# A fused attention and MLP kernel on one core: another recorded order of all instructions, from other planning constants

## The chip, the cores and the metric

One Trainium2 chip, one of its cores. The metric is device microseconds of one execution; the kernel before was executed three times (707.9, 707.91 and 710.89 us, median 707.91). The profile is of one more execution of 703.5 us, whose span from the first to the last instruction is 701.8 us.

## The reference, cut to what matters

Two stages in float32. A recurrence over 768 tokens for 4 x 8 heads of dimension 40:

```python
for t in range(S):
    y[:, :, t] = einsum('bhd,bhde->bhe', r_t, state)
    Sa = einsum('bhde,bhe->bhd', state, a_t)
    state = state * w_t[:, :, None, :] - einsum('bhd,bhe->bhde', Sa, b_t) + einsum('bhd,bhe->bhde', v_t, k_t)
```

and on its output, as 3072 tokens of 320 numbers, a bilinear MLP: `((x @ w1) * (x @ w2)) @ w3 @ w_out`, with `w1`, `w2` of 320 x 1024, `w3` of 1024 x 1024 and `w_out` of 1024 x 320. The weights come as float64.

## The kernel before, in words

The 768 tokens are cut into 12 chunks of 64 (numbered 0 to 11), and the 32 heads into two groups of 16. A chunk goes through these steps, each a function:

- `load` brings the decays and keys (tile `fm`, four buffers: two chunks) and `a` (tile `lh`). `scale` forms running products of the decays (a scan, L441), their inverses, and multiplies them into `lh` (L453) and into `fm` (L465).
- `causal` makes the products of all pairs of tokens (L490) and masks them with GpSimd selects (L508). `solve` inverts a triangular system on VectorE: pairs of a product (L548) and a reduction (L552), some 19 us in a row for a chunk. `join` puts the inverse together with two TensorE steps, L623 and L630; between them ScalarE copies the first result (`JP`).
- `pairs` (L667, and GpSimd selects L677) and `tokens` (L694) prepare the other operands.
- `rec` carries the state over a chunk, for each group: TensorE L718 and L725, then L733, four VectorE products L738, TensorE L745, VectorE L771 (state) and L790 (output), TensorE L778 (the state turned round for the next chunk).
- `gather` moves the output into the layout of the MLP by twelve DMAs, and `mlp` runs 24 TensorE units for a chunk: 16 of 8 matmuls (L842) and 8 of 6 (L868), each near 1 us. VectorE splits the input (`xs`, L828) and multiplies (L856); the low part `gl` (L859) is made on VectorE or GpSimd.

Before any `mlp` all weights have to be converted: 31 `convert` calls on VectorE (L333, L337, L341 each), `split` into high and low parts (L382, L394, on GpSimd), and `product`, which folds `w3` and `w_out` into one matrix on TensorE (L404). The first `mlp` reads the key `W12`, which is written when all of `w1` and `w2` are split.

The order of the work is not that of the code. Every step is recorded by `op(engine, cost, due, fn, r, w, two=...)`: the planned cost, a due time, what it reads and writes. `Order.place` then places all operations by a list schedule: on each engine the operation that could start first by the plan, among equals the one due first; on TensorE, among those within `sl` of the first, the one with the smallest due time, less `kp` when it needs no change of the array's mode. `two=True` marks operations of VectorE and GpSimd that the plan lets run only one at a time. The recorded closures are then called in the placed order, and each engine works through its own list in that order. The due times come from the numbers `T0`, `T` and `P`; `ON` says chunk by chunk whether L453 (`lh`), L465 (`xs`) and L859 (`gl`) run on GpSimd (`p`) or on VectorE (`d`). A cost in the plan is no wait on the chip: it only sets the order.

## Time and profile before

| | |
|---|---|
| median of 3 executions | 707.91 us |
| profiled execution | 703.5 us, span 701.8 us |
| TensorE busy | 588.2 us (84%) |
| VectorE busy | 562.1 us (80%) |
| ScalarE busy | 427.6 us (61%) |
| GpSimd busy | 199.5 us (28%) |
| mean granted TensorE clock | 0.952 |

TensorE is busy for a small part of the first 80 us, while VectorE is nearly full from 20 us on; from about 200 us on both are nearly full, and in the last 70 us only TensorE is. A busy share over the whole span therefore says little; the kernel has to be read stage by stage.

### The profile page before, as it was taken

To read this page: it belongs to the slowest core of one execution; us is meant where nothing else is said; L and a number is where in the kernel's file an instruction comes from. 1 tells how busy PE (TensorE), PEld (TensorE's weight loads), DVE (VectorE), ACT (ScalarE), POOL (GpSimd) and SP (SyncE) were. 2 spreads that over 40 slices of the span, in tenths; PEclk is the share of its full clock that TensorE was granted. 3 is DMA by queue.
4 is the path that set the end of the run, shared out by engine and by line. 5 is a ranking of instruction groups with operands and counts; after the bars stand their busy time and mean duration, and the time that the engine had idled before them with its cause. 6 is when DMAs were issued, how large, how long until landed. Compare 5 with 4: busy or idle time off the path is not lost.

```text
span 701.8 us, 22309 instructions
## 1 busy us (share of the span) xinstructions
PE 588.2 (84%) x9458; PEld 522.5 (74%) x9458; DVE 562.1 (80%) x989; ACT 427.6 (61%) x927; POOL 199.5 (28%) x186
## 2 busy tenths in 40 slices
PE   1331597475899799998999899999899999999996
PEld 1321475244798698897988889889888999899996
DVE  7899899989899888979979879699697797963321
ACT  2781575648567386693694765856848569464231
POOL 4370214204240010330221632426427143200200
PEclk9999998785899899998999999999999899999999
DMA  7940575152331321413314313233133250210011
GB/s 177 227 125 23 183 193 149 60 161 79 75 71 43 80 69 53 104 44 90 85 40 104 71 48 84 69 99 88 34 95 71 50 127 22 64 32 22 21 24 23
DMA packets 61090, 57.56 MB, mean 82 GB/s; under 512 B 29560, under 2 KB 52600, under 8 KB 60984
## 3 DMA queue, kind: packets, MB, share of 16 engines
q1 hardware_dynamic: 60984, 56.07, 31.4%
q8 instruction: 76, 1.25, 0.8%
q14 instruction: 30, 0.25, 0.1%
HBM read 47.40 MB, written 3.93 MB: 73 GB/s over the span
## 4 chain that ended last, share of the span: by engine, by line
DVE 47%; PE 29%; DMA 10%; ACT 6%; issue 6%; SPq 1%; POOL 1%; DVEq 0%; ACTq 0%; POOLq 0%
PE bank L842 12%; DVE tmp L548 8%; DMA fm<-in_fmx_dram 8%; DVE xu L738 6%; PE bank L868 5%; DVE mf L337 3%; DVE fm L441 3%; DVE ab L552 3%; DVE DG L552 2%; ACT JP L212 2%; DVE ab L522 2%; DVE Tp L552 2%; PE bank L745 2%; ACT TT L212 2%; PE bank L725 2%
## 5 line engine op out<-in xcount | busy, mean ns | idle before, releaser
L842 PE MATMUL bank<-xs,W 128*128 128x256 f32 x1536 | 207.4, 289 | 0.9 <-ACT TT L212 0.7
L842 PEld LDWEIGHTS bank<-xs,W 128*128 128x128 f32 x1536 | 189.4, 191 | 8.3 <-issue 1.8
L677 POOL TENSOR_SCALAR_AFFINE_SELECT xu<-xu 64x512 f32<-64x512 f32 x48 | 33.9, 707 | 176.5 <-ACT xu L212 168.9
L212 ACT ACTIVATE xu<-bank 64x256 f32<-64x256 f32 (+2 forms) x184 | 70.8, 436 | 11.2 <-PE bank L667 5.0
L856 DVE TENSOR_TENSOR ga<-bank,ga 128x512 f32<-128x512 f32 x48 | 32.9, 687 | 54.3 <-PE bank L842 39.6
L212 ACT ACTIVATE JP<-bank 32x512 f32<-32x512 f32 x120 | 60.4, 503 | 11.4 <-PE bank L490 7.0
L508 POOL TENSOR_SCALAR_AFFINE_SELECT lh<-lh 64x512 f32<-64x512 f32 x48 | 35.7, 744 | 108.8 <-ACT lh L212 105.9
L868 PE MATMUL bank<-W3h,gh 128*128 128x320 f32 x192 | 62.7, 327 | 0.0
L745 PE MATMUL bank<-xu,bk 128*40 128x104 f32 (+1 forms) x768 | 51.8, 271 | 12.3 <-DVE xu L738 11.7
L404 PE MATMUL bank<-wof,w3f 128*128 128x320 f32 x128 | 45.0, 508 | 18.8 <-DVE w3f L341 18.8
L738 DVE TENSOR_TENSOR xu<-bank,mask_h 64x416 f32<-64x416 f32 x96 | 56.2, 585 | 4.4 <-PE bank L733 2.1
L868 PE MATMUL bank<-W3l,gh 128*128 128x320 f32 x192 | 59.6, 310 | 0.0
L868 PE MATMUL bank<-W3h,gl 128*128 128x320 f32 x192 | 59.3, 309 | 0.0
L453 POOL TENSOR_TENSOR lh<-lh,fm 104x1024 f32<-104x1024 f32 x20 | 43.9, 2194 | 46.3 <-DVE fm L441 39.1
L745 PEld LDWEIGHTS bank<-xu,bk 128*40 128x40 f32 (+1 forms) x768 | 39.8, 125 | 22.8 <-DVE xu L738 19.3
L725 PE MATMUL bank<-xu,lh 104*64 104x104 f32 (+2 forms) x768 | 44.1, 267 | 11.8 <-POOL xu L677 7.2
L490 PE MATMUL bank<-lh,fm 40*64 40x64 f32 x1536 | 33.1, 244 | 22.7 <-DVE fm L465 14.5
L404 PEld LDWEIGHTS bank<-wof,w3f 128*128 128x128 f32 x128 | 27.7, 225 | 32.8 <-DVE w3f L341 15.2
L725 PEld LDWEIGHTS bank<-xu,lh 104*64 104x64 f32 (+2 forms) x768 | 38.0, 144 | 17.0 <-POOL xu L677 7.8
L490 PEld LDWEIGHTS bank<-lh,fm 40*64 40x64 f32 x1536 | 29.7, 157 | 27.3 <-issue 22.5
L859 POOL TENSOR_TENSOR gl<-ga,gh 128x512 fp32r<-128x512 f32 x24 | 32.6, 1360 | 60.8 <-ACT gh L212 60.8
L212 ACT ACTIVATE SB<-bank 40x320 f32<-40x320 f32 x44 | 18.9, 429 | 50.8 <-PE bank L778 50.3
(99 smaller groups left out, 1223.6 us busy)
## 6 DMA issues: line engine op xcount, KB each, us to landing
fm<-in_fmx_dram SPq DMA_DIRECT2D x24, 627.2 KB
raw<-in_w3t_dram SPq DMA_DIRECT2D x16, 512.0 KB
rv<-in_rv_dram SPq DMA_DIRECT2D x48, 160.0 KB
raw<-in_w_dram SPq DMA_DIRECT2D x8, 512.0 KB
lh<-in_fma_dram SPq DMA_DIRECT2D x48, 80.0 KB
xu<-in_vt_dram SPq DMA_DIRECT2D x48, 80.0 KB
out_dram<-o SPq DMA_DIRECT2D x48, 80.0 KB
xr<-y SPq DMA_DIRECT2D x72, 40.0 KB
```

Source lines behind the costliest of these rows:

```text
L212: act.activation(out_, in_, AF.Copy, scale=scale)
L404: pe.matmul(out=pt.t[:, 0:DM], lhsT=w[:, j], rhs=wof[:, j], start=(j == 0), stop=(j == NJ - 1))
L453: e.tensor_tensor(out=lh.t[0:104], in0=lh.t[0:104], in1=gam(c, g)[:, :, 0:C].unsqueeze(1).to_broadcast(full), op=ALU.mult)
L490: pe.matmul(out=bank(ab)[64 * x:64 * x + 64, p], lhsT=X[r, p, x], rhs=lh.t[r, ab, p], start=True, stop=True)
L508: pool.affine_select(out=lh.t[q, ab], in_=lh.t[q, ab], pattern=[[0, NP], [1, C]], compare_op=ALU.is_gt, fill=0.0, base=0, channel_multipli ...
L548: dve.tensor_tensor(out=scratch(*shape), in0=x().to_broadcast([128, *shape]), in1=y().to_broadcast([128, *shape]), op=ALU.mult)
L552: dve.tensor_reduce(out=out_(), in_=scratch(*shape), axis=mybir.AxisListType.X, op=ALU.add)
L725: pe.matmul(out=view(hp[h])[64 * ab:64 * ab + 64, u], lhsT=lh.t[k, ab, HP * h + u], rhs=xu.t[k, ab, HP * h + u], start=True, stop=True)
L738: dve.tensor_tensor(out=xu.t[64 * ab:64 * ab + 64, ab, k:NP:2], in0=view(us[ab])[r], in1=mask_h[r].unsqueeze(1).to_broadcast([64, HP, N]), ...
L745: pe.matmul(out=q(r, p), lhsT=bk.t[:, p, r], rhs=xu.t[:, ab, p], start=(c == 0), stop=True, skip_group_check=True)
L842: pe.matmul(out=pt.t[:, TOK * x:TOK * x + TOK], lhsT=WT[k][:, cs], rhs=xs.t[:, z], start=(n == 0), stop=(n == 7))
L868: pe.matmul(out=pt.t[:, 0:DM], lhsT=l.t[:, j, ts], rhs=W3[r][:, j], start=(j == 0 and n == 0), stop=(j == NJ - 1 and n == 2))
```

## The change

Only numbers and marks that the plan reads; no operation is added or removed. The due times and the choice of engine:

```diff
-T0, T = 44.72, 43.86
-P = dict(w0=17.72, ws=3.55, ld=127.38, sc=59.49, ca=49.87, so=11.77, sp=31.26, jo=5.02, pa=19.94, tk=0.13, rg=7.05,
-         ga=24.69, ml=80.68, kp=7.95, mt=26.56, mg=18.0, sl=0.28, kw=0.05)
+T0, T = 51.29, 43.14
+P = dict(w0=24.52, ws=3.55, ld=120.72, sc=65.76, ca=50.03, so=18.07, sp=32.97, jo=0, pa=14.07, tk=0, rg=6.24,
+         ga=21.36, ml=83.8, kp=5.81, mt=26.61, mg=18.52, sl=0.56, kw=2.39)
 
-ON = dict(ws="p", lh="pppddppppppp", xs="dpppdpdpdppd", gl="ddddpppppdpd")
+ON = dict(ws="p", lh="pdpddppdpppp", xs="dpppdpdpdddp", gl="pdpdppppdpdp")
```

Planned costs of some twenty operations move by a few per cent, the product of the first seven `solve` pairs gets a factor, and the two GpSimd selects lose their mark:

```diff
-            op("pool", 0.83, due + 6, f3, w=[(lh, ab)], two=True)
+            op("pool", 0.67, due + 6, f3, w=[(lh, ab)])
...
-            steps.append((0.16 + n / 960, f1, False))
+            steps.append((0.15 + slow * n / 960, f1, False))
...
-                 lambda s=s: A8(s).unsqueeze(2), (4, n, n))
+                 lambda s=s: A8(s).unsqueeze(2), (4, n, n), 1.75)
...
-            op("pool", 0.85, due + 2, lambda q=q, ab=ab: pool.affine_select(
+            op("pool", 0.67, due + 2, lambda q=q, ab=ab: pool.affine_select(
...
-                fill=0.0, base=0, channel_multiplier=-1), w=[(xu, "g", ab)], two=True)
+                fill=0.0, base=0, channel_multiplier=-1), w=[(xu, "g", ab)])
```

Counted over the 12 chunks, `ON` moves the `lh` products from 20 on GpSimd and 4 on VectorE to 16 and 8, the `xs` products from 14 and 10 to 12 and 12, and the `gl` subtractions from 24 and 24 to 32 and 16.

What that does to the order, at three places. First VectorE around the last weight conversion (the last L341). Before, that conversion stands ahead of all VectorE work of chunk 1's recurrence (L738, L771, L790):

```order
L333 TENSOR_SCALAR mf_145<-raw_141 128x512
L337 SCALAR_TENSOR_TENSOR mf_145<-raw_141,mf_145 128x512
L341 SCALAR_TENSOR_TENSOR mf_145<-raw_141,mf_145 128x512
L738 TENSOR_TENSOR xu_105<-bank_134,mask_h 64x4x104
L738 TENSOR_TENSOR xu_105<-bank_131,mask_h 64x4x104
```

Now the first group's share of that recurrence stands ahead of the last two conversions (the last one begins in the last row here):

```order
L738 TENSOR_TENSOR xu_105<-bank_131,mask_h 64x4x104
L738 TENSOR_TENSOR xu_105<-bank_130,mask_h 64x4x104
L738 TENSOR_TENSOR xu_105<-bank_131,mask_h 64x4x104
L738 TENSOR_TENSOR xu_105<-bank_130,mask_h 64x4x104
L564 TENSOR_TENSOR tmp<-DG 128x128
L333 TENSOR_SCALAR mf_146<-raw_140 128x512
...
L771 TENSOR_TENSOR st_110<-bank_132,fm_94 104x160
L790 TENSOR_TENSOR y_111<-bank_132,fm_94 104x4x64
...
L333 TENSOR_SCALAR mf_145<-raw_141 128x512
```

Counted over the whole list up to the last L341, nothing moved behind it, and two L453 (chunk 1's), four L738, two L771, two L790 and nine steps of chunk 2's `solve` moved ahead of it. Up to the first L828, the `xs` split that the first MLP needs, again nothing moved behind, and what moved ahead is two L453, four L738, two L771, two L790, five L548 and five L552 of `solve`, and one L436, one L441 and one L453 of chunk 3. On TensorE all of chunk 1's recurrence and the preparation of chunk 2 (L667, L694) now stand ahead of the first L842.

Second, TensorE in the recurrence of chunk 2, first group. Before, L745 follows L733 at once, though the four VectorE products L738 stand between them:

```order
L725 MATMUL bank5_135<-xu0_105,lh0_96 64x104 x8
L733 MATMUL bank2_132<-hs0_109,TT0_115 64x104
...
L733 MATMUL bank4_134<-hs0_109,TT0_115 64x104
L745 MATMUL bank0_130<-xu0_105,bk0_107 40x104 x8
L745 MATMUL bank1_131<-xu0_105,bk0_107 40x104 x8
L778 MATMUL bank3_133<-ident_64,st0_110 40x104 x4
```

Now three MLP units (18 L868) stand between them:

```order
L725 MATMUL bank5_135<-xu0_105,lh0_96 64x104 x8
L842 MATMUL bank2_132<-xs0_1519,W12_0_89 128x256 x2
...
L733 MATMUL bank4_134<-hs0_109,TT0_115 64x104
L868 MATMUL bank5_135<-W3h_87,gh0_1517 128x320
...
L868 MATMUL bank5_135<-W3h_87,gl0_1518 128x320
L745 MATMUL bank0_130<-xu0_105,bk0_107 40x104 x8
L745 MATMUL bank3_133<-xu0_105,bk0_107 40x104 x8
```

From chunk 2 on every group of every chunk has at least three other pieces there now; before, the first groups of chunks 2 and 4 had none.

Third, TensorE in `join` of chunk 6. Before, L630 follows L623 at once (in chunks 8 and 9 too):

```order
L842 MATMUL bank4_134<-xs0_1403,W12_4_1153 128x256 x2
L623 MATMUL bank0_130<-TDX0_102,JP0_113 32x32 x32
L630 MATMUL bank0_130<-TDX0_102,JP0_113 32x32 x32
L842 MATMUL bank5_135<-xs0_1403,W12_0_89 128x256 x2
L842 MATMUL bank5_135<-xs0_1403,W12_2_90 128x256
```

Now three MLP units stand between the two steps:

```order
L623 MATMUL bank2_132<-TDX0_102,JP0_113 32x32 x32
L842 MATMUL bank5_135<-xs0_1519,W12_0_89 128x256 x2
...
L842 MATMUL bank5_135<-xs0_1519,W12_4_1229 128x256 x2
L868 MATMUL bank0_130<-W3h_87,gh0_1517 128x320
...
L868 MATMUL bank0_130<-W3h_87,gl0_1518 128x320
L630 MATMUL bank2_132<-TDX0_102,JP0_113 32x32 x32
```

No chunk from 2 on has the two steps side by side any more. At the end of the list TensorE runs 48 MLP units behind the last L745 now, 41 before.

## Rows read from the trace of the kernel before

**Rows 1.** The page of the profile: the span, and two engines' busy tenths in 40 equal slices.
```profile
span 701.8 us, 22309 instructions
...
PE   1331597475899799998999899999899999999996
...
DVE  7899899989899888979979879699697797963321
```

**Rows 2.** The table of stretches: length, then busy us (instructions) of PE, PEld, DVE, ACT and POOL, the granted clock, the DMA share and GB/s.
```profile
160.00:180.00 20.00, 13.45 (x193) 10.65 (x194) 18.06 (x37) 14.74 (x30) 8.87 (x7) 0.50 0.17 52
300.00:350.00 50.00, 47.60 (x799) 43.06 (x798) 42.60 (x80) 31.85 (x68) 12.47 (x11) 0.93 0.29 67
```

**Rows 3.** VectorE in order of time, 182 to 197 us: start, length, then the instruction, and in brackets the idle time before it. The first row is the first MLP's `xs`, the others are steps of `solve`.
```profile
181.97 0.96 DVE L828 TENSOR_TENSOR xs<-xr,xs 128x768 fp32r<-128x768 f32 x1 [0.26 <-ACT xs L825]
182.84 0.41 DVE L548 TENSOR_TENSOR tmp<-Tp,ab 128x256 f32<-128x256 f32 x1
183.29 0.43 DVE L552 TENSOR_REDUCE ab<-tmp 128x32 f32<-128x256 f32 x1
186.50 0.69 DVE L548 TENSOR_TENSOR tmp<-Tp,ab 128x512 f32<-128x512 f32 x1
```

**Rows 4.** TensorE in order of time from the first MLP unit on. Of the eight rows up to 207 us that belong to chunk 1's recurrence and chunk 2's preparation (L733, L745, L778, L667, L694) the first and the last are shown.
```profile
186.11 1.21 PE L842 MATMUL bank<-xs,W 128*128 128x256 f32 x8
187.25 0.94 PE L733 MATMUL bank<-hs,TT 64*64 64x104 f32 x32
...
206.04 0.57 PE L694 MATMUL bank<-ident,fm 104*128 104x104 f32 x4
```

**Rows 5.** Groups of instructions by line: busy us and mean ns of one, then the idle time before them.
```profile
L453 POOL TENSOR_TENSOR lh<-lh,fm 104x1024 f32<-104x1024 f32 x20 | 43.9, 2194 | 46.3 <-DVE fm L441 39.1 <-issue 3.6 <-DMA xr<-y 3.3
L859 POOL TENSOR_TENSOR gl<-ga,gh 128x512 fp32r<-128x512 f32 x24 | 32.6, 1360 | 60.8 <-ACT gh L212 60.8
L465 DVE TENSOR_TENSOR fm<-fm,gi 104x1024 f32<-104x1024 f32 x10 | 12.2, 1223 | 0.3
L859 DVE TENSOR_TENSOR gl<-ga,gh 128x512 fp32r<-128x512 f32 x24 | 16.8, 700 | 11.5 <-ACT gh L212 11.5
L738 DVE TENSOR_TENSOR xu<-bank,mask_h 64x416 f32<-64x416 f32 x96 | 56.2, 585 | 4.4 <-PE bank L733 2.1
L790 DVE TENSOR_TENSOR y<-bank,fm 104x256 f32<-104x256 f32 x48 | 19.1, 416 | 3.2 <-PE bank L745 3.2
L771 DVE TENSOR_TENSOR st<-bank,fm 104x160 f32<-104x160 f32 x44 | 13.5, 318 | 3.0 <-PE bank L745 2.9
L436 DVE TENSOR_SCALAR_CACHE_REDUCE fm<-fm 104x520 f32<-104x520 f32 x24 | 16.6, 691 | 12.6 <-DMA fm<-in_fmx_dram 12.5
L337 DVE SCALAR_TENSOR_TENSOR mf<-raw,mf 128x512 uint32<-128x512 uint32 x31 | 29.9, 964 | 1.0
L571 DVE TENSOR_TENSOR Tp<-tmp,DG 128x128 f32<-128x128 f32 x12 | 9.3, 779 | 0.4
L441 DVE TENSOR_TENSOR_SCAN fm<-fm,first 104x520 f32<-104x520 f32 x24 | 36.1, 1505 | 0.6
```

**Rows 6.** VectorE in order of time, 39 to 52 us, and two later rows of lines met there.
```profile
39.56 1.02 DVE L461 SCALAR_TENSOR_TENSOR gi<-gt,gi 104x512 f32<-104x512 f32 x1
40.50 7.36 DVE L441 TENSOR_TENSOR_SCAN fm<-fm,first 104x520 f32<-104x520 f32 x1
48.79 2.98 DVE L571 TENSOR_TENSOR Tp<-tmp,DG 128x128 f32<-128x128 f32 x1
...
75.76 0.69 DVE L337 SCALAR_TENSOR_TENSOR mf<-raw,mf 128x512 uint32<-128x512 uint32 x1
...
181.31 0.40 DVE L571 TENSOR_TENSOR Tp<-tmp,DG 128x128 f32<-128x128 f32 x1
188.65 1.24 DVE L441 TENSOR_TENSOR_SCAN fm<-fm,first 104x520 f32<-104x520 f32 x1
```

**Rows 7.** GpSimd in order of time, 39 to 52 us.
```profile
39.05 2.04 POOL L677 TENSOR_SCALAR_AFFINE_SELECT xu<-xu 64x512 f32<-64x512 f32 x2
...
42.29 2.16 POOL L453 TENSOR_TENSOR lh<-lh,fm 104x1024 f32<-104x1024 f32 x1
...
49.37 2.15 POOL L453 TENSOR_TENSOR lh<-lh,fm 104x1024 f32<-104x1024 f32 x1
```

**Rows 8.** TensorE in order of time: the rows behind 210 us with an idle time of over a microsecond before them.
```profile
232.29 4.51 PE L745 MATMUL bank<-xu,bk 128*40 128x104 f32 x32 [4.26 <-DVE xu L738]
323.77 4.51 PE L745 MATMUL bank<-xu,bk 128*40 128x104 f32 x32 [2.08 <-DVE xu L738]
402.93 1.20 PE L630 MATMUL bank<-TDX,JP 32*32 32x32 f32 x64 [1.96 <-ACT JP L212]
448.49 1.20 PE L630 MATMUL bank<-TDX,JP 32*32 32x32 f32 x64 [1.48 <-ACT JP L212]
495.16 1.20 PE L630 MATMUL bank<-TDX,JP 32*32 32x32 f32 x64 [1.74 <-ACT JP L212]
539.82 1.20 PE L630 MATMUL bank<-TDX,JP 32*32 32x32 f32 x64 [1.54 <-ACT JP L212]
```

**Rows 9.** The table of stretches again (columns as in rows 2), for the four stretches behind 200 us with a granted clock of 0.50.
```profile
231.30:238.10 6.80, 5.65 (x50) 3.92 (x54) 5.90 (x12) 0.43 (x1) 0.00 (x0) 0.50 0.03 5
...
323.50:330.30 6.80, 6.37 (x42) 4.94 (x43) 6.03 (x16) 0.00 (x0) 0.00 (x0) 0.50 0.10 15
...
449.80:453.20 3.40, 3.40 (x72) 3.17 (x75) 1.45 (x2) 2.23 (x5) 1.06 (x1) 0.50 0.00 0
...
541.90:548.70 6.80, 6.80 (x113) 6.32 (x111) 1.03 (x2) 5.96 (x13) 1.30 (x2) 0.50 0.11 33
```

**Rows 10.** The chain that ended last, its end: start, length, piece.
```profile
657.84 8.68 PE bank L842 x72
666.52 7.05 PE bank L868 x48
673.56 15.24 PE bank L842 x128
688.81 7.06 PE bank L868 x48
```

More of the change, by code (lines that the diff above doesn't have):

```diff
@@ L342, in f6 @@
                                      op0=ALU.logical_shift_right, op1=ALU.bitwise_or)
-        op("sp", 0.4, due - 8, f1, w=[raw], dma=2.0)
-        op("act", 0.72, due, f2, r=[raw], w=[sq])
-        op("act", 0.72, due, f3, w=[sq])
-        op("dve", 0.52, due, f4, r=[raw], w=[mf], two=True)
-        op("dve", 0.72, due, f5, r=[raw], w=[mf], two=True)
-        op("dve", 0.74, due, f6, r=[raw, "conv"], w=[mf] if dst is None else [mf, *w], two=True)
+        op("sp", 0.35, due - 8, f1, w=[raw], dma=2.5)
+        op("act", 0.8, due, f2, r=[raw], w=[sq])
+        op("act", 0.76, due, f3, w=[sq])
+        op("dve", 0.42, due, f4, r=[raw], w=[mf], two=True)
+        op("dve", 0.7, due, f5, r=[raw], w=[mf], two=True)
+        op("dve", 0.7, due, f6, r=[raw, "conv"], w=[mf] if dst is None else [mf, *w], two=True)
         return mf
@@ L384, in split @@
             op("act", 0.65, due, lambda: copy(WT[k][:, cs], mf.t.bitcast(F32)), r=[mf, *over], w=[("W", k, f)])
-            both(ON["ws"], 1.35, 0.62, due, f2, r=[mf, *over], w=[("W", k, f)])
+            both(ON["ws"], 1.28, 0.69, due, f2, r=[mf, *over], w=[("W", k, f)])
             return due
@@ L393, in split @@
                    r=[mf, *over], w=[key])
-            both(ON["ws"], 1.35, 0.62, due, lambda e, q=q, dst=dst: e.tensor_tensor(
+            both(ON["ws"], 1.28, 0.69, due, lambda e, q=q, dst=dst: e.tensor_tensor(
                 out=WT[4][64:128, dst], in0=mf.t[q].bitcast(F32), in1=WT[4][q, dst], op=ALU.subtract), r=[mf, *over], w=[key])
@@ L408, in product @@
         op("act", 0.45, due, lambda: copy(W3[0][:, ib], pt.t[:, 0:DM]), r=[pt], w=[("W3", ib)])
-        op("dve", 0.43, due, lambda: dve.tensor_tensor(out=W3[1][:, ib], in0=pt.t[:, 0:DM], in1=W3[0][:, ib],
+        op("dve", 0.48, due, lambda: dve.tensor_tensor(out=W3[1][:, ib], in0=pt.t[:, 0:DM], in1=W3[0][:, ib],
                                                      op=ALU.subtract), r=[pt], w=[("W3", ib)])
@@ L423, in load @@
         fm, lh = fm_[c, g], lh_[c, g] = slot("fm"), slot("lh")
-        op("sp", 0.4, due, lambda: sp.dma_start(out=fm.t, in_=fmx[c, g]), w=[(fm, "g"), (fm, "x")], dma=2.5)
+        op("sp", 0.4, due, lambda: sp.dma_start(out=fm.t, in_=fmx[c, g]), w=[(fm, "g"), (fm, "x")], dma=3.0)
         for ab in range(2):
@@ L468, in scale @@
         op("dve", 0.7, due, f1, w=[G])
-        op("dve", 1.26, due, f2, w=[G], two=True)
+        op("dve", 1.24, due, f2, w=[G], two=True)
         op("act", 0.63, due + 1, f3, r=[G], w=[gi])
-        op("act", 0.71, due + 1, f4, w=[gi])
-        both(ON["lh"][c], 2.35, 1.16, due + 1, f5, r=[G], w=[(lh, 0), (lh, 1)])
+        op("act", 0.76, due + 1, f4, w=[gi])
+        both(ON["lh"][c], 2.2, 1.22, due + 1, f5, r=[G], w=[(lh, 0), (lh, 1)])
         op("dve", 0.71, due + 2, f6, r=[G, gi], w=[gt], two=True)
         op("dve", 0.73, due + 2, f7, r=[gt], w=[gi], two=True)
-        both(ON["xs"][c], 2.6, 1.16, due + 3, f8, r=[gi], w=[(fm, "x")])
+        both(ON["xs"][c], 2.38, 1.22, due + 3, f8, r=[gi], w=[(fm, "x")])
     def causal(c, g, due):
@@ L541, in scratch, with dots @@
             return tmp[:, 0:n].rearrange(f"p ({' '.join(names)}) -> p {' '.join(names)}", **dict(zip(names, shape)))
-        def dots(out_, x, y, shape):
+        def dots(out_, x, y, shape, slow=1.0):
             n = shape[0] * shape[1] * shape[2]
@@ L830, in mlp @@
         parts = [(xr, i) for i in range(12)] if first else []
-        op("act", 0.9, due - 3, f1, r=[*parts, "W12"], w=[(xs, "h")])
+        op("act", 0.98, due - 3, f1, r=[*parts, "W12"], w=[(xs, "h")])
         op("dve", 0.98, due - 2, f2, r=[(xs, "h"), *parts], w=[(xs, "l")], two=True)
@@ L855, in mlp @@
                 else:
-                    op("dve", 0.65, t, lambda a=a, pt=pt: dve.tensor_tensor(out=a.t, in0=wide(pt), in1=a.t, op=ALU.mult),
+                    op("dve", 0.69, t, lambda a=a, pt=pt: dve.tensor_tensor(out=a.t, in0=wide(pt), in1=a.t, op=ALU.mult),
                        r=[pt], w=[a])
             op("act", 0.64, t, lambda a=a, j=j: copy(gh.t[:, j:j + 2], a.t), r=[a], w=[(gh, j)])
-            both(ON["gl"][c % NCH], 1.35, 0.62, t + 1, lambda e, a=a, j=j: e.tensor_tensor(
+            both(ON["gl"][c % NCH], 1.3, 0.69, t + 1, lambda e, a=a, j=j: e.tensor_tensor(
                 out=gl.t[:, j:j + 2], in0=a.t, in1=gh.t[:, j:j + 2], op=ALU.subtract), r=[a, (gh, j)], w=[(gl, j)], of=op)
```

2 lines of the change are left out of this document (1 added, 1 removed).

## The prediction, made before the changed kernel ran

> **What bounds the kernel now.** The page comes first, its row of slices above all [rows 1]. In the first fifth VectorE is nearly full and TensorE mostly idle: the weights are being converted, and no MLP can start. From about 200 us on both are nearly full: 47.60 us of 50 on TensorE and 42.60 on VectorE between 300 and 350 us [rows 2]. In the last five slices only TensorE works. So the span is the time at which the first MLP unit starts (186.11 us [rows 4]), plus the TensorE work left by then, plus what TensorE loses after it, plus 6 us behind its last matmul. The chain of waits shows that the last MLPs run without a gap: 8.68 + 7.05 + 15.24 + 7.06 = 38.0 us up to 695.9 us [rows 10].
>
> What TensorE loses after the start is read from two views. In order of time, six rows have over a microsecond of idle before them: two before L745, which waits for the four L738 on VectorE, and four before L630, which waits for ScalarE's copy of L623's result: 4.26 + 2.08 + 1.96 + 1.48 + 1.74 + 1.54 = 13.1 us [rows 8]. The table of stretches shows the granted clock at 0.50, the lower of its two levels (1.2 of 2.4 GHz), four times, twice beginning in such a gap and twice some 2 us behind one [rows 8, 9]: 5.65 + 6.37 + 3.40 + 6.80 = 22.2 us of work that would take half of that, so 11.1 us lost. Together 24.2 us that hang on six gaps.
>
> **The change, part by part.** The work is the same; I go by which work stands ahead of which.
>
> *VectorE ahead of the first MLP.* What moved ahead of L828 is costed by kind. Two L453 of chunk 1 and one of chunk 3 at 1.22 us make 3.7 (the time is that of L465 on VectorE, also 104x1024, 1223 ns [rows 5]); four L738 at 0.585, two L771 at 0.318 and two L790 at 0.416 make 3.8 [rows 5]; one L436 0.69 [rows 5], one L441 1.24 [rows 6]; four `solve` pairs at 0.41 + 0.43 and one pair at about 0.69 + 0.69 make 4.7 [rows 3]. The sum is 14.1 us. Before, L828 starts at 181.97 [rows 3], on a VectorE that is busy 18.06 of 20 us just then [rows 2], so nothing hides this: L828 moves to 196.1, ends at 197.1, and since all TensorE work that stood behind the first unit now stands ahead of it, the first L842 comes at once: 197.1 instead of 186.1, **+11.0**.
>
> *TensorE ahead of the first MLP.* Chunk 1's recurrence and chunk 2's preparation lie behind 186.11 before, eight rows from 187.25 to 206.04 us [rows 4], 6.5 us in all, and now lie ahead of it, under VectorE: **-6.5**.
>
> *VectorE held by GpSimd.* An L441 takes 7.36 us while GpSimd runs product after product [rows 6, 7], and 1.24 alone [rows 6]; L571 takes 2.98 and 0.40 alone. By groups: L441 36.1 - 24 x 1.24 = 6.3, L571 9.3 - 12 x 0.40 = 4.5, L337 29.9 - 31 x 0.69 = 8.5 [rows 5, 6]: 19.3 us, nearly all ahead of the first MLP. Two L453 of chunk 1, 2.16 and 2.15 us, lie under exactly these two operations [rows 7]; `ON` takes both off GpSimd (VectorE's own time for them is in the 14.1). That gives 4.3 back (2.16 + 2.15). The eight other long products of that stretch stay, in other places. Bounds 0 and 19.3; I take 6, nearest to the two that are named: **-6**.
>
> *Selects without their mark.* The plan no longer keeps L508 and L677 apart from VectorE. An L461 beside selects takes 1.02 us [rows 6, 7], where the same-sized L337 takes 0.69 alone [rows 6]: 0.33 us for a meeting. There are 96 selects: 0 to 32 us. Most of VectorE's time in the plan is `solve`, whose rows keep their length; I take six more meetings that count: **+2**. The Trainium skill (SBUF — State Buffer, the section on the single rule of the shared port pair) says that this pair is an exclusive lock, held for a whole instruction, and that a VectorE operation with two SBUF inputs blocks until a GpSimd operation that reads SBUF has ended. By that rule a meeting would cost up to a whole select, half of the 2.04 us of a pair [rows 7], the six 6 us and not 2, and the forecast below would be 699.4; the row shows a third of that, and the row decides.
>
> *The gaps.* Three MLP units now stand between L733 and L745 in every group from chunk 2 on, near 3 us against the 4 x 0.585 = 2.3 us of L738 [rows 5], and no L630 follows L623 at once. If the cover holds, 24.2 us go. But VectorE, 42.60 of 50 us busy [rows 2], has to deliver in a shorter time: 24 us less over the 470 us from 186 to 658 us makes 85% into 90%, with a list in fixed order that waits for TensorE, ScalarE and loads on its way. And chunk 7's gap of 1.48 us stood there although L630 did not follow L623 at once. So some gaps come back elsewhere, and a gap can take the clock with it. Bounds: 24.2 given back wholly or not at all; I take 11 back, a little under half: **-13**.
>
> *Engine moves by `ON`.* Four L453 and two L465 come to VectorE, 6 x 1.22 = 7.3; eight `gl` at 0.70 leave it, 5.6 [rows 5]: +1.7 us of 562, of which two L453 are counted above. GpSimd loses 4 x 2.19 and two L465 and gains 8 x 1.36 [rows 5]; it is idle most of the time. The last chunk's `gl` goes to GpSimd: 1.36 for 0.70, at most 0.7 us at the very end, and L868 work covers it: 0. In SP's list conversions' loads go ahead of some of chunk 0's; VectorE is already full behind 20 us, so 0. The 48 units at the end instead of 41 are the same work in another place: 0.
>
> Sum: 11.0 - 6.5 - 6 + 2 - 13 = **-12.5 us** on the profiled 703.5, so 691.0. That execution lies 4.4 us under the median of 707.9; on the median the forecast is **695.4**.
>
> **The rivals.** *VectorE takes over* (same). The start costs 4.5, the stalls return 6, and every gap that is closed reopens somewhere because VectorE comes late: 11.0 - 6.5 - 6 + 2 = +0.5, 708.4. For it: L745's gaps are waits for VectorE, and VectorE had 85%. Against it: four of six gaps were waits for ScalarE behind a missing cover.
>
> *The MLP starts late and it is never made up* (slower). The place is L828, 14.1 us of VectorE work later. If the long products hold VectorE as before (no return) and the gaps only move, the time is 11.0 - 6.5 + 2 = +6.5, so 714.4. The point: the first L842 later than 197 with the idle behind it as large as before. For it: the converted weights come later by the order itself. Against it: the two worst stalls lose their partner.
>
> *All of it comes through* (much faster). Fifteen us of stalls go, and only 5 us of gaps return: 11.0 - 6.5 - 15 + 2 - 19 = -27.5, 680.4.
>
> *The plan does not do what it is for.* The diff has no line on the clock; only due times, marks and costs. Then the gaps would be where they were. The order speaks against it: the covers are there.
>
> **How the numbers follow.** A measurement of this kernel tells about 0.5% (3.5 us) from no change: 704.4 to 711.4 is the same. The forecast has 0.48, all of it 0.17, VectorE takes over 0.17, the late start 0.18 (0.02 of it still within the bound). Faster 0.65, same 0.19, slower 0.16. The forecast's own range is 687 to 703 (8 us either way: half of the stall term and half of the gap term). To leave out no more than 2 in 10, the range goes to 679 below, which takes in most of the third rival, and to 712 above, which takes in the first and the edge of the second.
>
> **What would show it.** In the changed profile: the first L842 near 193 us (197.1 - 6 + 2), against 186.11 before; L453 eight times on VectorE; the mean of L337 under 964 ns and of L441 under 1505 ns; no row of over a microsecond before L630 and fewer before L745; less than 22 us at a clock of 0.50 behind the start; 45 us of L842 and L868 without a gap at the end. It is wrong if L828 starts at 196 or later, or if TensorE's idle behind the first L842 is as large as before: then the order only moved the waits.

## The result, and the profile after

The changed kernel takes 677.32 us (median of four executions, 675.84 to 678.05) against 708.57 us of the kernel before beside it: a ratio of 0.9551, 95% interval 0.9521 to 0.958. The forecast of 695.4 us had the direction, and its range, 679 to 712, does not reach the result. The profiled execution took 677.89 us, with a span of 676.2 us and a granted clock of 0.975.

The page of the changed kernel, its span and the busy tenths of TensorE and VectorE in 40 slices, as in [rows 1]:

```profile
span 676.2 us, 22337 instructions
...
PE   1422996768799999898999989899999989999996
...
DVE  7999999999999799798799798898987997914310
```

VectorE stands at 9 for twelve slices in a row, where before 8 and 9 alternate. So the start is where to look first: VectorE's list up to the first MLP's `xs` (L828) as one stretch, from its first `scale` operation at 7.38 us to the start of L828 (length, then busy us of PE, PEld, DVE, ACT and POOL, clock, DMA share, GB/s). Before:

```profile
7.38:181.97 174.59, 97.37 (x1316) 72.74 (x1320) 158.45 (x257) 106.91 (x258) 54.74 (x42) 0.88 0.48 133
```

After:

```profile
7.38:169.53 162.15, 100.30 (x1489) 75.55 (x1489) 152.55 (x281) 114.11 (x274) 54.32 (x42) 0.94 0.56 152
```

VectorE does 24 more instructions there, 14.1 us of work by the forecast's count, and yet is busy 5.9 us less: 158.45 + 14.1 - 152.55 = 20.0 us of its busy time were no work of these lists. Row by row, against the shortest row of the same form, the time for which VectorE's operations were held falls from 30.7 to 13.1 us, 17.7 less; most of the other 2.3 is that neighbouring rows overlap 2.0 us more. Its idle time falls too, from 174.59 - 158.45 = 16.1 to 162.15 - 152.55 = 9.6 us. So 14.1 - 20.0 - 6.5 = -12.4 us, from 181.97 [rows 3] to 169.53. The idle part is read from VectorE's waits up to L828 (releaser, us in total, times, longest). Before:

```profile
DVE fm L436 <- DMA fm<-in_fmx_dram: 5.7, 2, 3.9
DVE W3l L409 <- ACT W3h L212: 1.8, 2, 1.3
```

After:

```profile
DVE fm L436 <- DMA fm<-in_fmx_dram: 1.9, 3, 1.4
```

Most of it is one wait. The fourth load of `fm` is issued at 7.06 us before and at 7.02 now; before, VectorE's list came to its L436 too early, now other work stands ahead of it, as VectorE's rows before and after show:

```profile
20.16 0.69 DVE L436 TENSOR_SCALAR_CACHE_REDUCE fm<-fm 104x520 f32<-104x520 f32 x1 [3.89 <-DMA fm<-in_fmx_dram]
...
34.67 0.69 DVE L436 TENSOR_SCALAR_CACHE_REDUCE fm<-fm 104x520 f32<-104x520 f32 x1
```

The held part is read from the groups by line, as in [rows 5] (busy us, mean ns, idle before):

```profile
L441 DVE TENSOR_TENSOR_SCAN fm<-fm,first 104x520 f32<-104x520 f32 x24 | 30.9, 1287 | 0.6
L337 DVE SCALAR_TENSOR_TENSOR mf<-raw,mf 128x512 uint32<-128x512 uint32 x31 | 22.4, 724 | 1.0
...
L571 DVE TENSOR_TENSOR Tp<-tmp,DG 128x128 f32<-128x128 f32 x12 | 4.9, 404 | 0.4
```

L441 falls from 1505 to 1287 ns, L337 from 964 to 724, L571 from 779 to 404. Those three give back (36.1 - 30.9) + (29.9 - 22.4) + (9.3 - 4.9) = 17.1 of the 19.3 us that stood as the upper bound. The stretch of [rows 6], again in order of time on VectorE:

```profile
38.33 1.49 DVE L441 TENSOR_TENSOR_SCAN fm<-fm,first 104x520 f32<-104x520 f32 x1
...
40.17 1.02 DVE L337 SCALAR_TENSOR_TENSOR mf<-raw,mf 128x512 uint32<-128x512 uint32 x1
...
47.17 0.39 DVE L571 TENSOR_TENSOR Tp<-tmp,DG 128x128 f32<-128x128 f32 x1
```

and on GpSimd, as in [rows 7]:

```profile
34.93 2.35 POOL L465 TENSOR_TENSOR fm<-fm,gi 104x1024 f32<-104x1024 f32 x1
37.35 3.30 POOL L677 TENSOR_SCALAR_AFFINE_SELECT xu<-xu 64x512 f32<-64x512 f32 x3
```

The long product L465 now runs beside the short first steps of `solve`, and ends at 37.28 us, before the L441 begins; that L441 meets selects instead of a subtraction and two products and takes 1.49 us, not 7.36.

TensorE around the first MLP unit, as in [rows 4]:

```profile
168.77 0.93 PE L694 MATMUL bank<-ident,fm 104*128 104x104 f32 x8
169.48 0.36 PE L842 MATMUL bank<-xs,W 128*128 128x256 f32 x1
170.54 2.63 PE L842 MATMUL bank<-xs,W 128*128 128x256 f32 x20 [0.70 <-DVE xs L828]
```

Chunk 1's recurrence and chunk 2's preparation lie ahead of it, and it comes with L828 at once. The first L842 stands 16.6 us earlier (186.11 to 169.48), where the forecast had it 7 us later.

Behind it the forecast had expected most, and there is least. TensorE's rows behind 171 us with over a microsecond of idle before them, as in [rows 8]:

```profile
182.56 1.26 PE L490 MATMUL bank<-lh,fm 40*64 40x64 f32 x64 [1.96 <-POOL fm L465]
187.04 1.20 PE L623 MATMUL bank<-TDX,JP 32*32 32x32 f32 x64 [1.13 <-DVE TDX L600]
275.49 1.26 PE L490 MATMUL bank<-lh,fm 40*64 40x64 f32 x64 [2.66 <-POOL fm L465]
315.93 1.28 PE L490 MATMUL bank<-lh,fm 40*64 40x64 f32 x64 [1.33 <-ACT bk L212]
434.21 0.41 PE L868 MATMUL bank<-W3h,gh 128*128 128x320 f32 x1 [1.13 <-DVE xu L738]
514.09 1.31 PE L490 MATMUL bank<-lh,fm 40*64 40x64 f32 x64 [1.42 <-issue]
548.19 1.26 PE L490 MATMUL bank<-lh,fm 40*64 40x64 f32 x64 [1.15 <-POOL fm L465]
```

All six gaps of before are gone, and seven others stand there, most of them before L490. The stretches at half clock, as in [rows 9], are three of them, 10.3 us together:

```profile
188.90:192.30 3.40, 3.40 (x51) 3.17 (x51) 2.99 (x13) 2.49 (x5) 0.00 (x0) 0.50 0.00 0
277.60:281.10 3.50, 3.50 (x33) 3.44 (x28) 2.16 (x3) 3.38 (x7) 0.28 (x1) 0.51 0.00 0
318.60:322.00 3.40, 3.40 (x18) 3.40 (x17) 2.09 (x3) 3.26 (x8) 2.52 (x2) 0.50 0.17 48
```

The end of the chain, as in [rows 10], is 15.26 + 7.05 + 15.24 + 7.06 = 44.6 us without a gap.

From the first L842 to the last L868 it is 695.9 - 186.1 = 509.8 us before and 670.0 - 169.5 = 500.5 us after: 9.3 less, of which 6.5 are the TensorE work that moved ahead. TensorE's idle time in that stretch, added up from its rows, is 21.8 us before and 23.2 after.

### The profile page after: what moved, and what is told of

It is laid out like the page before. It is cut to its first block, busy times and chain, and to the rows that moved or that the text cites. A ratio compares the mean times of both kernels' runs of the same rounds, so it can differ in the third digit from the quotient of the medians.

```text
span 676.2 us, 22337 instructions
## 1 busy us (share of the span) xinstructions
PE 577.7 (85%) x9458; PEld 515.3 (76%) x9458; DVE 551.4 (82%) x987; ACT 431.8 (64%) x927; POOL 211.9 (31%) x188
## 4 chain that ended last, share of the span: by engine, by line
DVE 47%; PE 32%; ACT 8%; issue 6%; DMA 4%; POOL 1%; DVEq 0%; SPq 0%; POOLq 0%
PE bank L842 14%; DVE tmp L548 9%; DVE xu L738 6%; PE bank L868 5%; DMA fm<-in_fmx_dram 4%; DVE ab L552 3%; DVE mf L337 3%; ACT JP L212 3%; DVE Tp L552 3%; PE bank L745 2%; DVE fm L441 2%; DVE ab L522 2%; PE bank L725 2%; PE bank L490 2%; DVE w3f L341 2%
## 5 line engine op out<-in xcount | busy, mean ns | idle before, releaser
L842 PE MATMUL bank<-xs,W 128*128 128x256 f32 x1536 | 204.8, 289 | 0.7 <-DVE xs L828 0.7
L842 PEld LDWEIGHTS bank<-xs,W 128*128 128x128 f32 x1536 | 190.3, 193 | 5.8 <-DVE xs L828 0.9
L677 POOL TENSOR_SCALAR_AFFINE_SELECT xu<-xu 64x512 f32<-64x512 f32 x48 | 46.0, 958 | 187.9 <-ACT xu L212 172.1
L859 POOL TENSOR_TENSOR gl<-ga,gh 128x512 fp32r<-128x512 f32 x32 | 41.0, 1283 | 109.8 <-ACT gh L212 109.8
L490 PE MATMUL bank<-lh,fm 40*64 40x64 f32 x1536 | 32.7, 236 | 45.0 <-POOL fm L465 23.3
L738 DVE TENSOR_TENSOR xu<-bank,mask_h 64x416 f32<-64x416 f32 x96 | 56.3, 587 | 14.0 <-PE bank L733 12.0
L490 PEld LDWEIGHTS bank<-lh,fm 40*64 40x64 f32 x1536 | 29.5, 149 | 49.4 <-POOL fm L465 25.9
L508 POOL TENSOR_SCALAR_AFFINE_SELECT lh<-lh 64x512 f32<-64x512 f32 x48 | 41.0, 853 | 76.8 <-ACT lh L212 73.9
L856 DVE TENSOR_TENSOR ga<-bank,ga 128x512 f32<-128x512 f32 x48 | 32.8, 683 | 39.1 <-PE bank L842 30.3
L868 PE MATMUL bank<-W3h,gh 128*128 128x320 f32 x192 | 63.1, 329 | 1.1 <-DVE xu L738 1.1
L868 PE MATMUL bank<-W3l,gh 128*128 128x320 f32 x192 | 59.2, 309 | 0.0
L868 PE MATMUL bank<-W3h,gl 128*128 128x320 f32 x192 | 59.2, 308 | 0.0
L404 PE MATMUL bank<-wof,w3f 128*128 128x320 f32 x128 | 41.7, 479 | 16.7 <-DVE w3f L341 16.7
L745 PE MATMUL bank<-xu,bk 128*40 128x104 f32 (+1 forms) x768 | 47.5, 262 | 5.9 <-DVE xu L738 5.8
L212 ACT ACTIVATE gh<-ga 128x512 fp32r<-128x512 f32 x48 | 30.3, 631 | 34.6 <-DVE ga L856 34.2
L725 PE MATMUL bank<-xu,lh 128*64 128x104 f32 (+2 forms) x768 | 43.4, 266 | 9.5 <-ACT xu L212 5.8
L453 POOL TENSOR_TENSOR lh<-lh,fm 104x1024 f32<-104x1024 f32 x16 | 35.4, 2216 | 48.4 <-DVE fm L441 22.3
L745 PEld LDWEIGHTS bank<-xu,bk 128*40 128x40 f32 (+1 forms) x768 | 37.5, 120 | 14.7 <-DVE xu L738 12.1
L725 PEld LDWEIGHTS bank<-xu,lh 128*64 128x64 f32 (+2 forms) x768 | 37.6, 144 | 14.2 <-ACT xu L212 6.9
```

The source lines that it names most:

```text
L212: act.activation(out_, in_, AF.Copy, scale=scale)
L404: pe.matmul(out=pt.t[:, 0:DM], lhsT=w[:, j], rhs=wof[:, j], start=(j == 0), stop=(j == NJ - 1))
L490: pe.matmul(out=bank(ab)[64 * x:64 * x + 64, p], lhsT=X[r, p, x], rhs=lh.t[r, ab, p], start=True, stop=True)
L508: pool.affine_select(out=lh.t[q, ab], in_=lh.t[q, ab], pattern=[[0, NP], [1, C]], compare_op=ALU.is_gt, fill=0.0, base=0, channel_multipli ...
L677: op("pool", 0.67, due + 2, lambda q=q, ab=ab: pool.affine_select(out=xu.t[q, ab, :, 0:C], in_=xu.t[q, ab, :, 0:C], pattern=[[0, NP], [1, ...
L725: pe.matmul(out=view(hp[h])[64 * ab:64 * ab + 64, u], lhsT=lh.t[k, ab, HP * h + u], rhs=xu.t[k, ab, HP * h + u], start=True, stop=True)
```

## The experiments

The theory after the result: the gain lies ahead of the first MLP unit, and comes from products on GpSimd that no longer hold VectorE. The first rival: it lies behind it, in the covered gaps and the clock, as the forecast's sum had it. A second rival: the choice of engines does it, not the order.

Several kernels carry a written order. Every recorded operation has a number; `Order.place` takes a list of them instead of choosing, with the same choice of buffers, and `both` takes the engine from a set (the first line below stands for the code that is replaced):

```diff
-        (its choice of the next operation by start and due time)
+        for n in SEQ:
+            o = ops[n]
...
+        on = "p" if len(order.ops) in GP else "d"
```

In the first four kernels this list stands at the top of the file, so their line numbers are 75 higher: L917 is L842 of the others, L820 is L745, L705 is L630, L516 is L441, L646 is L571. Where the text below names TensorE's idle time or the time at half clock, it is between the first L842 and the last L868.

### Each half of the order alone

`SEQ` is the new order up to the first MLP unit and the order of before for all the rest, with each part's engines.

> The changed order up to its first MLP unit on TensorE (694 of 2970 operations), from there on the order of before for all that is left. Theory A (the gain lies ahead of the first MLP unit, where VectorE no longer stands behind GpSimd's products): first L842 near 171 us, and TensorE's losses behind it stay at some 30 us, so 22 us under before, about 687 us. Rival B (the gain lies behind it, in the covers between L733 and L745 and between L623 and L630): about 703 us, 5 us under before.

Measured: 683.96 us, ratio 0.9664 (0.959 to 0.9738). The first L842 starts at 169.13 us, and the gaps of before are back, as TensorE in order of time shows:

```profile
169.13 0.36 PE L917 MATMUL bank<-xs,W 128*128 128x256 f32 x1
...
210.50 0.37 PE L820 MATMUL bank<-xu,bk 128*40 128x104 f32 x2 [4.09 <-DVE xu L813]
...
380.36 1.20 PE L705 MATMUL bank<-TDX,JP 32*32 32x32 f32 x64 [1.74 <-ACT JP L286]
```

The other way round: the start of before, and the new order behind it.

> The order of before up to its first MLP unit on TensorE (654 operations), then the changed order for all that is left. Theory A: first L842 near 186 us, some 5 us under before, about 703 us. Rival B: the covers are all there, 20 us under before, about 688 us.

Measured: 704.9 us, ratio 0.9914 (0.9867 to 0.996). L828 stands at 181.50 us, L337 means 964 ns as before, and from the first L842 to the last L868 it is 499.7 us, as in the new kernel and 10.0 less than before. But that first L842 stands at 194.90, behind the TensorE work that the new order puts ahead of it: 8.8 us later than before, which takes most of the 10.0 back. By the ratios, three quarters of the gain come with the start (3.4% of 4.5%), one quarter with the rest.

### The products on GpSimd

The order of before, unchanged, with the products of chunks 1 and 2 (four L453, four L465) on VectorE:

```diff
-GP = {..., 475, 478, 492, 495, ..., 704, 707, 721, 724, ...}
+GP = {..., ...}
```

> The order of before, operation by operation, with the eight products L453 and L465 of chunks 1 and 2 on VectorE instead of GpSimd, each at its old place in the order. It adds 8 x 1.22 = 9.8 us of work to VectorE. If GpSimd's products hold VectorE there (19.3 us of stretched L441, L571 and L337), VectorE reaches L828 some 8 us earlier, L337's mean falls from 964 to about 700 ns, and the time is about 700 us. If the stretched rows have another cause (selects, loads), they stay and the time rises by up to 9.8 us to about 718 us.

Measured: 699.66 us, ratio 0.9838 (0.9755 to 0.9922). VectorE has 8 x 1.22 = 9.8 us more work ahead of L828, and L828 starts at 171.59 us, 10.4 earlier. In order of time on VectorE, L441 and L571 of [rows 6]:

```profile
39.88 2.93 DVE L516 TENSOR_TENSOR_SCAN fm<-fm,first 104x520 f32<-104x520 f32 x1
43.75 0.83 DVE L646 TENSOR_TENSOR Tp<-tmp,DG 128x128 f32<-128x128 f32 x1
```

2.93 for 7.36 and 0.83 for 2.98. VectorE's busy time up to L828 falls from 158.45 to 150.16 us in spite of the 9.8 us of work, so the eight had held it for 18.1 us: 2.3 us each, more than the 1.22 us of doing the product itself. The other direction: the new order, unchanged, with chunk 1's two L453 back on GpSimd.

```diff
-GP = {..., 478, 495, ...}
+GP = {..., 475, 478, 492, 495, ...}
```

> The changed order, operation by operation, with chunk 1's two L453 back on GpSimd, each at its place in the order. If taking these two off GpSimd (the marks in ON) is what ended the stalls, stalls of at least 4.3 us return against 2.4 us of VectorE work that goes: about 679 us or more, and VectorE rows stretched by 2 us are back. If the place of the products in the order is what counts, no long stall returns and the time is 675 to 677 us.

Measured: 680.73 us, ratio 0.9619 (0.9561 to 0.9677), first L842 at 168.93. The time is that of the first expectation, and two stretched rows are back: one of 2.96 us at 21.67 (L333 there), and (L416 is L341)

```profile
42.22 2.54 DVE L416 SCALAR_TENSOR_TENSOR mf<-raw,mf 128x512 uint32<-128x512 uint32 x1
```

But the start is no later: what these two hold is about what VectorE saves by not doing them. Behind the start the profiled execution has 502.3 us for 500.5, and the interval overlaps that of the new kernel. So the new order with the old choice of engines up to the first MLP unit starts its MLP 17.2 us earlier than before: that is the order's, and the two marks in `ON`, which the forecast had priced at 4.3 us, add nothing to the start. And the new order with its own six GpSimd products of chunks 1 and 2 on VectorE:

```diff
-GP = {..., 478, 495, ..., 704, 707, 721, 724, ...}
+GP = {..., ...}
```

> The changed order, operation by operation, with the six products (L453, L465) that it has on GpSimd for chunks 1 and 2 on VectorE, each at its place in the order: the counterpart of moving eight in the order of before, which gained 1.6%. If the changed order has hidden them beside VectorE work that does not wait for GpSimd, all of 6 x 1.22 = 7.3 us comes on top ahead of the first MLP unit: first L842 near 177 us, about 684 us. If they still held VectorE there, the time stays near 677 us or falls.

Measured: 685.92 us, ratio 0.9752 (0.9685 to 0.9819); the first L842 starts at 175.56, 6.1 us later, where 6 x 1.22 = 7.3 us of work were added. In the old order moving products to VectorE is worth 1.6%, in the new one it costs about as much as the work itself. So in the new order these six lie where they hold nearly nothing. Where a product lies beside work that it holds, as in the old order, changing its engine helps too; what helped in this change is the new place.

### The three parts of the diff

Costs and marks alone (the diff's second block and the other planned costs), in the kernel before:

```diff
-            op("pool", 0.83, due + 6, f3, w=[(lh, ab)], two=True)
+            op("pool", 0.67, due + 6, f3, w=[(lh, ab)])
...
-        both(ON["lh"][c], 2.35, 1.16, due + 1, f5, r=[G], w=[(lh, 0), (lh, 1)])
+        both(ON["lh"][c], 2.2, 1.22, due + 1, f5, r=[G], w=[(lh, 0), (lh, 1)])
```

> The kernel before with the changed planned costs and marks alone (T0, T, P and ON as before), planned anew. Theory A1 (the products met the conversions because the old costs made the plan drift from the chip: conversions planned at 1.98 us and run in 1.8, the first products of solve planned too short; with the new costs they meet solve as planned): L337's mean falls from 964 to about 720 ns, first L842 near 175 us, about 692 us. Rival A2 (the due times do it): stalls stay, L337 near 960 ns, within 1% of before.

Due times alone (`T0`, `T` and `P` of the diff):

> The kernel before with the changed T0, T and P alone, planned anew. Theory A1 (the costs do it): the stalls stay, L337's mean near 960 ns, first L842 near 186 us, within 1% of before. Rival A2 (the due times do it): L337 near 720 ns, about 690 us.

Engines alone (`ON` of the diff):

> The kernel before with the changed ON alone, planned anew: two products L453 of chunk 1 leave GpSimd ahead of the first MLP, four gl subtractions a chunk change place later. Both A1 and A2 say that this is worth little: 2 to 5 us of the stalls, 704 to 708 us. A rival A3 (the engine choice does it) says 690 us or less.

And the new kernel without one of the three, each by the same lines turned round: without costs and marks,

> The changed kernel with the planned costs and marks of before, T0, T, P and ON as changed, planned anew. Alone, each of the three parts was worth under 1% (706, 701, 702 us), so they are now taken away one at a time. Theory C1 (the three were chosen together and each is needed: the gain is that of one particular order): about 698 us, VectorE's stretched rows ahead of the first MLP unit back to some 12 us from 6.4. Rival C2 (the costs hardly matter once the due times are right): within 1% of 677 us.

without due times,

> The changed kernel with T0, T and P of before, costs, marks and ON as changed, planned anew. Theory C1: about 700 us. Rival C3 (costs and engine choice carry it): within 1% of 677 us.

without engines,

> The changed kernel with ON of before, costs, marks and due times as changed, planned anew. Theory C1: about 695 us. Rival C4 (the engine choice hardly matters, as putting two products back in the same order showed: 680.7 us): within 1% of 677 us.

Measured against the kernel before:

| | alone | the change without it |
|---|---|---|
| costs and marks | 0.9992 (0.9948 to 1.0035) | 1.014 (1.0071 to 1.0209) |
| due times | 0.9906 (0.9864 to 0.9947) | 0.9938 (0.9875 to 1.0001) |
| engines | 0.9926 (0.9876 to 0.9976) | 0.9919 (0.9871 to 0.9968) |

The ratios alone multiply to 0.983; together they give 0.955. Costs and marks, worth nothing alone, are worth most in company: without them the other two are slower than before. A list schedule is no sum of its numbers; each row is one other order, and the 4.5% belong to the order that all three give. Costs alone bring the first L842 to 177.0 us and lose it behind it (524.1 us to the last L868, with 30.8 of idle). L337's mean is 900 ns there, not the 720 of theory A1. The same holds without the engines: 174.8 us, then 519.6 with 32.8 of idle. With the old costs and marks the start is late: 186.4 us with the engines alone, 185.5 with engines and due times. So the costs and marks bring the start forward, but only together with the other two does the time not go again behind it.

### The covers alone

The order of before, with MLP units on TensorE brought forward over the six gaps of [rows 8]: two ahead of L630 in chunks 6, 8 and 9, one more in chunk 7, two ahead of the first L745 of chunk 2 and three ahead of that of chunk 4. In chunk 6:

```
 L623 (chunk 6)
+L842 x8
+L842 x8
 L630 (chunk 6)
-L842 x8
-L842 x8
```

> The order of before, operation by operation, with the next MLP units of TensorE's list brought forward: two ahead of L630 in chunks 6, 8 and 9, one more in chunk 7, three ahead of the first L745 of chunk 4 and two ahead of that of chunk 2. If the six gaps and the half clock behind them are losses of their own, up to 24 us go, about 686 us. If the gaps only move because other engines come late then (as the 5 us of the changed order behind its first MLP unit suggest), 5 to 10 us go, about 701 us.

Measured: 708.79 us, ratio 1.0025 (0.9983 to 1.0067). The time at half clock falls from 23.9 to 6.8 us, and the kernel is no faster. TensorE in order of time, chunk 6:

```profile
398.80 1.20 PE L623 MATMUL bank<-TDX,JP 32*32 32x32 f32 x64
401.73 2.15 PE L842 MATMUL bank<-xs,W 128*128 128x256 f32 x16 [1.74 <-ACT JP L212]
```

and ScalarE there:

```profile
399.21 1.26 ACT L212 ACTIVATE TT<-TDX 32x512 f32<-32x512 f32 x2
400.49 1.19 ACT L212 ACTIVATE JP<-bank 32x512 f32<-32x512 f32 x2
```

The gap stands before L842 now, with the same releaser: ScalarE's `JP` copies come behind two `TT` copies and end at 401.68, and the trace shows the MLP unit waiting for them, though it does not read `JP`. By the trace's releaser what it lacks is the bank they free. The cover fills nothing, it queues behind the same copy. That is so for the four gaps at `JP` (6.9 us before, 6.4 now). The waits of L745 for L738 do shrink, from 8.9 to 5.9 us, but those of L725 for ScalarE grow from 1.2 to 3.7.

### What holds the idle time

Two theories remained for the gap term: VectorE, nearly full, gives the covered time back late (A), or steps in a fixed order do, whatever VectorE's load (B). Three kernels take work off VectorE from chunk 4 on, by summing over one element in the last seven products and reductions of each `solve`:

```diff
+            sh = [*shape[:2], 1] if c >= 4 and shape[0] >= 8 else shape; k = sh[2]
             def f1():
-                dve.tensor_tensor(out=scratch(*shape), in0=x().to_broadcast([128, *shape]),
-                                  in1=y().to_broadcast([128, *shape]), op=ALU.mult)
+                dve.tensor_tensor(out=scratch(*sh), in0=x()[:, :, :, 0:k].to_broadcast([128, *sh]),
+                                  in1=y()[:, :, :, 0:k].to_broadcast([128, *sh]), op=ALU.mult)
```

> The order before, unchanged in its sequence, with the same shortened `solve` from chunk 4 on. Theory A (VectorE's load makes the idle): the waits before L745 shrink, but the four before L630 stay, since L630 still follows L623 at once and waits for ScalarE: idle from 21.8 to some 14 to 18 us, time 700 to 705. Theory B (fixed chains): idle 20 us or more, time within 4 us of 708.

Measured: 703.12 us, ratio 0.9934 (0.9895 to 0.9974). The stretch 186 to 658 us of the kernel before (columns as above),

```profile
186.00:658.00 472.00, 450.16 (x7795) 409.84 (x7791) 384.95 (x705) 304.74 (x640) 135.19 (x120) 0.97 0.28 66
```

and of this one:

```profile
186.00:658.00 472.00, 449.75 (x7824) 410.67 (x7823) 330.07 (x704) 303.89 (x640) 135.26 (x120) 0.99 0.28 66
```

VectorE is busy 54.9 us less, and TensorE's idle is 472.00 - 449.75 = 22.3 us for 21.8. Neither of the two kinds of wait shrinks (8.9 and 6.9 us in the kernel before):

```profile
PE bank L745 <- DVE xu L738: 9.6, 16, 4.3
PE bank L630 <- ACT JP L212: 7.1, 5, 2.0
```

The idle is as B has it. The time is as A has it and just outside B's 4 us; it went with the time at half clock, 13.7 us for 23.9. Chunk 2's wait of 4.3 us is not tested: up to 236 us VectorE is as busy as before.

> The order before with the MLP units brought forward over six gaps (g1_covers_alone), and the same shortened `solve` from chunk 4 on. Theory A (in g1_covers_alone VectorE's load gave the covered time back): now the cover pays, 6 us or more under v2_old_order_short_solve, idle below 12 us. Theory B (the covers moved the wait to the bank that ScalarE's copy of L623 and the four copies ahead of it free, before L842): idle stays above 18 us, the rows before L842 that wait for JP stand as before, and the time is within 3 us of v2_old_order_short_solve.

Measured: 707.01 us, ratio 0.9995 (0.9953 to 1.0038), idle 23.7 us. TensorE's waits from 187 to 660 us (releaser, us in total, times, longest):

```profile
PE bank L842 <- ACT JP L212: 6.4, 4, 1.7
```

The covers are worth nothing with a lighter VectorE either (3.9 us slower than without them, just outside B's 3), and the wait for `JP` is the 6.4 us of the kernel with covers alone. In the old order the idle is B's.

> The new order, unchanged in its sequence; from chunk 4 on the last seven products and reductions of each `solve` (L548, L552) sum over one element instead of eight or four, so part of the inverse is left out. By the counts of elements and the rate of some 960 elements per us in the rows this takes near 5.7 us of VectorE work out of each of eight chunks, 46 us of some 420 behind the first MLP unit, and nothing of TensorE's. Theory A (TensorE's 23.2 us of idle behind the first unit are VectorE coming late, because it is nearly full): idle falls below 13 us, and the time by 8 us or more, to 670 or less. Theory B (the idle is made by steps in a fixed order: a product on GpSimd, a copy on ScalarE, a load, whatever VectorE's load): idle stays at 20 to 25 us, and the time within 4 us of 677.3.

Measured: 666.82 us, ratio 0.9431 (0.9363 to 0.9498), 10.5 us under the new kernel by the medians, 7.6 by the profiled executions; idle 17.2 us for 23.2. In the new order VectorE's load does hold some of it: the waits for L738 fall from 4.7 to 0.3 us, those for GpSimd's L465 stay. In the new kernel, then in this one:

```profile
PE bank L490 <- POOL fm L465: 6.7, 4, 2.7
...
PE bank L490 <- POOL fm L465: 6.5, 4, 2.6
```

That lies between the two theories: the time as A has it, 6 us of the idle, and 17 us that the load does not explain. The last kernel takes away two of those waits: the new order with four L465 (chunks 5 and 11) on VectorE.

```diff
-GP = {..., 1394, 1411, ..., 2768, 2785, ...}
+GP = {..., ...}
```

> The new order, unchanged in its sequence but for the engine of four products: both L465 of chunks 5 and 11 go from GpSimd to VectorE (four times 1.22 us there instead of 1.63 or more on GpSimd). The waits of L490 for them in the new trace are 2.66 us (at 272.8) and 1.15 us (at 547.0). If those waits are what they cost: 3 to 4 us less, near 674, and idle near 19.5 us. If TensorE's idle only moves, as the covers showed: 675 to 681, idle 22 to 25 us.

Measured: 684.35 us, ratio 0.9713 (0.9631 to 0.9796): 7.0 us slower than the new kernel, outside both expectations. TensorE in chunk 5 and chunk 11, in order of time:

```profile
276.12 2.10 PE L490 MATMUL bank<-lh,fm 40*64 40x64 f32 x64 [3.55 <-issue]
...
554.87 2.17 PE L842 MATMUL bank<-xs,W 128*128 128x256 f32 x16 [1.71 <-DVE ga L856]
...
559.62 1.20 PE L623 MATMUL bank<-TDX,JP 32*32 32x32 f32 x64 [1.69 <-DVE TDX L600]
```

and the clock behind the first of them:

```profile
274.60:284.90 10.30, 8.78 (x151) 8.63 (x152) 6.61 (x12) 7.78 (x14) 1.64 (x4) 0.50 0.01 2
```

The wait before L490 in chunk 5 grew from 2.66 to 3.55 us. The product ends no earlier on VectorE, where GpSimd's work beside it stretches it from 1.22 to 2.31 us:

```profile
273.60 2.31 DVE L465 TENSOR_TENSOR fm<-fm,gi 104x1024 f32<-104x1024 f32 x1
```

In chunk 11 the wait of 1.15 us is gone, a new one of 1.71 stands before L842, and that before L623 grew from 0.94 to 1.69. The time at half clock grew from 10.2 to 23.9 us, which at half the rate is 6.9 us. Between the first L842 and the last L868 TensorE's busy time grew by 4.9 us and its idle time by 2.0.

## Why the prediction was wrong

**VectorE ahead of the first MLP, +14.1 us of work: right.** The list has these 24 more instructions; added up from the rows, with the held time taken off, they are 13.7 us. That L842 would follow L828 at once was right too (0.70 us of wait).

**VectorE held by GpSimd, -6: the step that failed.** By VectorE's busy time it measured -20.0 with the selects' share and the closer rows in it, where the forecast had -6 + 2. Sorted by the GpSimd operation that ended inside the stretched row, products and subtractions held VectorE for 22.3 us ahead of L828 before, and for 3.8 now. The upper bound, 19.3, was worked out and then set aside: I returned only the two products that the diff names, and assumed that the eight others would hold VectorE as much in their new places. The kernels s1, s2 and r1 show that it depends on a product's place how much it holds; this order lays the products where they hold little. The rival that had this, 680.4, also needed 19 us from the gaps, and so stood at 0.17; that its time nearly came out is luck, for the gaps gave no such sum.

**VectorE's idle time ahead of the first MLP: no term in the sum.** I looked at the loads only, had VectorE full behind 20 us and gave 0. The wait that went most, 3.89 us, ends at 20.16 us, and it went because the waiting L436 moved in VectorE's own list, not because a load moved. Up to L828 VectorE waited 5.7 us for `fm` before and 1.9 after, and 1.8 before L409 that are gone; with smaller waits its idle fell by 6.5 us. 20.0 and 6.5 against 4 is 22.5 us, the distance of the first MLP unit, going on at 170.54, from the forecast's 193.

**TensorE ahead of the first MLP, -6.5: right** by its place in the list: it lies ahead of the first L842, under VectorE.

**The gaps, -13: wrong the other way.** From the start at 170.54 the TensorE stretch is 499.4 us, 10.3 less than before; 6.5 of them are moved work, so 3.8 are left for the whole term. The point that I had named for it came true: TensorE's idle is as large as before, 23.2 us for 21.8, while the six gaps and over half of the half clock went. The covers alone were worth nothing. Where the time went in the old order is shown for the four gaps before L630: the cover waits for the copy that the covered step waited for. What in the new order makes the 17 us that a lighter VectorE leaves is known by name only in part (6.5 of it before L490 for GpSimd); why no order with all its work went under 21.8 us stays open. VectorE's own rows are held for 16.4 us behind the first L828 now and for 5.5 before, by products and selects together; how much of that reached TensorE no run shows.

**Selects, +2: the row was misread.** Ahead of L828, stretched VectorE rows with a select ending inside them lose 3.2 us in 10 rows before and 3.6 in 11 now; behind it 1.9 us in 8 rows before and 6.8 in 23 now, and what these cost in time no run shows alone. The forecast measured a meeting against selects of some 1.02 us. A select alone takes 0.65; the longer ones had themselves waited. In the new kernel the second of the three selects of the stretch above takes 0.65 us and ends at 38.73. The L441 that begins at 38.33 ends 1.09 behind that, nearly its own length, and the third select, queued behind the L441, takes 1.86:

```profile
38.80 1.86 POOL L677 TENSOR_SCALAR_AFFINE_SELECT xu<-xu 64x512 f32<-64x512 f32 x1
```

So the 0.25 us by which that L441 is stretched, and the 0.33 us of an L461 or L337, are the rest of a select that was under way. That is what the rule of the Trainium skill (SBUF — State Buffer, the section on the single rule of the shared port pair) says, by which VectorE blocks until the GpSimd operation has ended: the trace agrees, and the row that the forecast set against the rule does not speak against it. With products the trace agrees as well: the L441 of 7.36 us [rows 6] met, beside the L453 of [rows 7], these two on GpSimd in the kernel before, back to back with it,

```profile
41.07 1.26 POOL L382 TENSOR_TENSOR W<-mf,W 128x512 fp32r<-128x512 f32 x1
...
44.42 2.34 POOL L465 TENSOR_TENSOR fm<-fm,gi 104x1024 f32<-104x1024 f32 x1
```

and ended at 47.86 us, 1.10 behind the last of them, which is nearly its own length: it was held through all three. Each of the three begins no later than the one before it ends; between the selects above lie 0.07 us, and there the L441 came in.

**Engine moves and the end, 0**: no L868 gap stands at the end (44.6 us), as said.

The start was off by 22.5 us one way and the gaps by 9.2 the other: 13.3 us, which takes the forecast of the profiled execution from 691.0 to 677.7, and it took 677.89. The other 4.4 us of the miss were added at the end, for the distance of the profiled execution before from the median; the changed kernel's profiled execution lies 0.6 us above its median. The range went down to 679 to take in most of the third rival, and so ended 2 us above the result.
